# Attention with relative bias, then a sine-gated MLP: 64-row score pairs on a planned PSUM tile, and an output turned by DMA

## The chip, the cores and the metric

The kernel runs on one core of a Trainium2 chip. The metric is the device time of one execution in microseconds, as the median of several runs. Engines are named as in the profile: PE (TensorE, matmuls), PEld (its weight loads), DVE (VectorE), ACT (ScalarE), POOL (GpSimd), SP (SyncE, which only issues DMAs here).

## The reference

Eight batches of 576 tokens with eight heads of 64. Attention adds a bias that depends on the distance of two tokens alone; the heads side by side are the 512 features of 4,608 tokens, which pass through an MLP of width 2,048:

```python
scores = scale * np.matmul(q, k.transpose(0, 1, 3, 2)) + bias
attn = np.exp(scores - scores.max(-1)); attn = attn / (attn.sum(-1) + 1e-9)
x = np.matmul(attn, v)            # to (4608, 512)
h = x @ w_in
s = np.sin(alpha * h)
out = (h + s * s / (alpha + 1e-09)) @ w_out
```

The bias is constant from distance 128 on. The kernel multiplies the exponentials by exp(bias minus that constant) in a window near the diagonal alone, and leaves the maximum out, since the row sum divides it away.

## The kernel before

**Stages.** For each batch t there is an attention stage (ACT holds the table of the exponential) and an MLP stage (the table of the sine); `set_table` (L788) loads 1.28 us of table between them. MLP works on blocks b of 512 tokens, which don't line up with batches of 576; the last stage does blocks 7 and 8.

**Order.** Nothing is scheduled by hand in the code below `Plan` (L55). `plan_pair`, `plan_av`, `plan_moe_in` and `plan_mo` add tasks with the engines that can do them, an estimated duration, dependences, a priority, and the buffers they take or use. `Plan.run` (L94) is a list scheduler in model time: it picks the next task and emits its instructions at once. So its choices are fixed when the program is built; each engine then works through its own queue in that order and waits on semaphores. Tasks marked `fill` (the second MLP matmul) go where PE has room, up to a quota in the attention stage.

**Scores (`plan_pair`, L565).** Heads go in pairs p = 0..3; k and q of a pair stand in partitions 0 to 63 and 64 to 127. The matmuls use all 128 rows: `kzs` holds the pair's k twice, each time with the other head's half zeroed, so that a product with both heads' q gives one head's scores. Keys are cut into four chunks of 128 and a rest of 64 (for the rest, `kts` puts both heads into one 128-column operand). Queries are cut into windows w of 384 and 192 (`WIN`). A pair has seven units: four of 2 x 384 columns, one of 2 x 288 (the rest) and two of 4 x 192. A unit fills two PSUM banks (`new_sc(2)`); one ACT exponential (L606) takes it to `u` in SBUF. DVE multiplies the bias windows in (L618, L635).

**Output (`plan_av`, L646).** For each pair and window, per 128 queries 9 matmuls with `u` as weights and v as moving operand (65 columns per head, the 65th being ones, so that the row sum comes along; 130 for the rest keys). DVE divides (L677, L678) into `xn`, PE turns each 128x128 piece (L688), and DVE or ACT copies it to `xT` (L698), the MLP's operand: features in partitions, a ring of 1,536 tokens.

**MLP.** `plan_moe_in`: 16 times per block, 4 matmuls of 512 columns from `w_in` into a bank of `sc` (L720), sine on ACT (L727), its square on ACT or DVE (L734, L736), and the gate on DVE (L741) into `g`. `plan_mo`: 4 times 16 matmuls of `g` and `w_out` into `mo`, a copy to `outs`, and a store from SP (L782).

**PSUM.** Eight banks: four for `sc` (scores and h in turn), two `av` (output and its turn), two `mo`.

**Loads.** For t of 2 and more, POOL's queue copies k and q from fp32 to fp16 in DRAM (`stage_kq`, L332, two batches ahead), SP's queue loads them transposed (`load_kqT`, L339): k to `kraw`, from there with four more DMAs to `kzs` and `kts`, then q. v comes through POOL's queue (`load_v16`). These are emitted by `first` (L799) at the head of an attention stage, but SP and POOL run ahead as far as their waits let them. For batches 0 and 1, PE turns k and q (`plan_tr`, L498), and DVE or ACT copies them out (L494, L496), k in two halves.

All operations' helpers are at one line each: `full` (L408) issues nearly every matmul.

Of the kernel before, what the change touches and what calls it, by code (L numbers as in the profile page):

```python
# [33 lines left out]
LAT = {"PE": 0.2, "ACT": 0.18, "DVE": 0.18, "POOL": 0.2, "DMA": 0.0}  # L34
NBUF = {"sc": 4, "av": 2, "mo": 2, "u": 2, "g": 2, "s16": 3, "sq": 3, "outs": 5, "xn": 3}


class Task:
    def __init__(self, engs, emit, deps, pri, nb=0.0):
        self.engs, self.emit, self.deps, self.pri, self.nb = engs, emit, list(deps), pri, nb  # L40
        self.allocs = []
        self.s_only = self.fill = False
        self.end = self.eng = None


class Buf:
    def __init__(self, tag):
        self.tag, self.users = tag, []

# [5 lines left out]
class Plan:  # L55


    def __init__(self):
        self.tasks = []
        self.sin = self.in_qk = False  # L60
        self.used = self.share = 0
        self.warm = None
        self.rings = {k: [] for k in NBUF}

    def add(self, engs, emit, deps=(), pri=0, nb=0.0, new=(), use=(), after=()):
        t = Task(engs, emit, deps, pri, nb)
        t.after = list(after)
        t.allocs = list(new)
        for b in list(new) + list(use):
            b.users.append(t)  # L70
        self.tasks.append(t)
        return t

    def ready(self, t):
# [8 lines left out]
        taken = {}  # L83
        for b in t.allocs:
            ring, n = self.rings[b.tag], NBUF[b.tag]
            k = taken[b.tag] = taken.get(b.tag, -1) + 1
            if len(ring) + k >= n:
                for x in ring[k - n].users:
                    if x.end is None:
                        return None  # L90
                    r = max(r, x.end)
        return r

    def run(self, t0):  # L94
        free = {e: t0 for e in ("PE", "ACT", "DVE", "POOL")}
        todo = list(self.tasks)
        while todo:
# [3 lines left out]
            for t in todo:  # L101
# [6 lines left out]
                for e in t.engs:  # L108
# [3 lines left out]
                    if t.fill:  # L112
                        if self.in_qk and self.used >= OFFSET + QUOTA * self.share:
                            continue
                        cands[e].append((st + FILL_GAP, t))
                    else:
                        cands[e].append((st, t))
            for e, c in cands.items():
# [6 lines left out]
                if best is None or (st, fin) < best[:2]:  # L125
                    best = (st, fin, e, t)
            st, fin, e, t = best
            if e == "PE" and self.warm is not None and free[e] < WARM_END:
                ring = self.rings["mo"][-2:]
                b = Buf("mo")  # L130
                x = Task({}, None, [], 0)
                b.users.append(x)
                if st > free[e] + 0.5 and len(ring) == 2 and all(
                    y.end is not None and y.end <= free[e] for y in ring[0].users
                ):
                    self.warm()
                    free[e] += 0.43
                    x.end, x.eng = free[e], e
                    self.rings["mo"].append(b)
                    continue  # L140
            if t.fill:
                self.used += 1
                st -= FILL_GAP
                fin -= FILL_GAP
            for b in t.allocs:
                self.rings[b.tag].append(b)
            t.emit(e)
            t.end, t.eng = fin + LAT[e], e
            free[e] = fin
# [6 lines left out]
FILL_GAP = 0.0  # L156
QUOTA = 48
# [15 lines left out]
SLACK = {"PE": 0.02, "ACT": 0.02, "DVE": 0.02, "POOL": 0.02}  # L173
# [14 lines left out]
def kernel(  # L188
# [24 lines left out]
    XN = 1536  # L213
# [21 lines left out]
    kzs = [sgl.tile([128, NP, 2 * S], F16, name=f"kz{i}") for i in range(2)]  # L235
    kraw = sgl.tile([128, NP, S], F16, name="kraw")
# [52 lines left out]
    def new_u():  # L289
        return tp.tile([128, 9, S], F16, name="u", tag="u", bufs=NBUF["u"])  # L290
# [16 lines left out]
    banks = [0]  # L307
    halves = {}

    def new_sc(n):  # L310
        z = banks[0] // 2 % 2
        m, pool = halves.get(z, (0, None))
        if m != n:
            if pool is not None:
                pool.release()
            pool = tc.alloc_tile_pool(
                name=f"sc{banks[0]}", bufs=1, space=bass.MemoryType.PSUM,
                side="right" if z else "left", reuse_waits="tile",
            )
            halves[z] = (n, pool)  # L320
        banks[0] += n
        if n == 1:
            return pool.tile([128, 512], F32, name="sc", tag="sc", bufs=2)
        return pool.tile([128, 2, 512], F32, name="sc", tag="sc", bufs=1)

    def new_av():
        return ps.tile([128, 512], F32, name="av", tag="av", bufs=NBUF["av"])

    def new_mo():
        return ps.tile([128, 512], F32, name="mo", tag="mo", bufs=NBUF["mo"])  # L330
# [8 lines left out]
    def load_kqT(t):  # L339
        nc.sync.dma_start_transpose(out=kraw[:, :, :], in_=staged_k.ap()[t])  # L340
        kz = kzs[t % 2]
        nc.sync.dma_start(out=kz[0:64, :, 0:S], in_=kraw[0:64, :, :])
        nc.sync.dma_start(out=kz[64:128, :, S : 2 * S], in_=kraw[64:128, :, :])
        for z in range(2):
            r = slice(64 * z, 64 * z + 64)
            nc.sync.dma_start(out=kts[t % 2][r, :, r], in_=kraw[r, :, 512:S])
        nc.sync.dma_start_transpose(out=qTs[t % 2][:, :, :], in_=staged_q.ap()[t])
# [48 lines left out]
    def clear(eng, i):  # L396
        eng.memset(kzs[i][0:64, :, S : 2 * S], 0.0)
        eng.memset(kzs[i][64:128, :, 0:S], 0.0)
# [11 lines left out]
    def warm(n):  # L410
        x = new_mo()
        for _ in range(n):
            full(x, zz[:, 0:128], zz, True, True)
# [51 lines left out]
    eps_ = new_mo()  # L465
# [21 lines left out]
    plan.warm = lambda: warm(1)  # L487
# [10 lines left out]
    def plan_tr(t, p, kq, pri, nb, deps=()):  # L498
# [3 lines left out]
        def mm(e):  # L502
            c.v = new_mo().bitcast(F16)
# [15 lines left out]
        def cp(e):  # L519
            pin = c.v[:, 0:S].rearrange("d (i p) -> d p i", i=SI)  # L520

            def put(dst, r):
                copy_on(e, dst.rearrange("d (p i) -> d p i", i=SI)[r], pin[r])

            if kq == 1:
                put(qTs[t][:, p, :], slice(0, 128))
            else:
                put(kzs[t][:, p, 0:S], slice(0, 64))
                put(kzs[t][:, p, S : 2 * S], slice(64, 128))

        m = plan.add({"PE": 0.4 if t == 0 and p == 0 else 0.5}, mm, deps, pri, nb, new=[b])
        eng = {"DVE": 0.75, "ACT": 0.72} if kq else {"DVE": 1.6, "ACT": 1.55}
        if t == 0:
            eng = {"ACT": 0.72} if p == 0 and kq else {"DVE": eng["DVE"]}
# [4 lines left out]
        def tail(e):  # L539
            for z in range(2):  # L540
                r = slice(64 * z, 64 * z + 64)
                nc.vector.tensor_copy(  # L542
                    out=kts[t][r, p, r], in_=kzs[t][r, p, S * z + 512 : S * z + S]
# [4 lines left out]
    def plan_alpha():  # L548
        b, c = Buf("mo"), Cell()

        def mm(e):
            c.v = new_mo()
# [12 lines left out]
    def plan_pair(t, p, kqt, tails, first, gate, ub):  # L565

        u = Cell()
        done = {}
        units = [(0, c) for c in range(4)] + [(1, 0), (2, 0), (2, 2)]
        head = []  # L570
        for i, (kind, c) in enumerate(units):
            b, sc = [Buf("sc"), Buf("sc")], Cell()

            def qk(e, i=i, kind=kind, c=c, sc=sc):
                if i == 0:
                    if p == 0:
# [3 lines left out]
                plan.share = (len(units) * p + i + 1) / (NP * len(units))  # L580
                if p == NP - 1 and i == len(units) - 1:
                    plan.in_qk = False
                sc.v = new_sc(2)
                kz, qT = kzs[t % 2], qTs[t % 2]
                for z in range(2):
                    if kind == 1:
                        full(sc.v[:, z, 0:288], kts[t % 2][:, p, :],
                             qT[:, p, 288 * z : 288 * z + 288], True, True)
                        continue
                    for y in range(1 if kind == 0 else 2):  # L590
                        k0 = S * z + 128 * (c + y)
                        q0, n = WIN[0 if kind == 0 else 1]
                        full(sc.v[:, z, n * y : n * y + n], kz[:, p, k0 : k0 + 128],
                             qT[:, p, q0 : q0 + n], True, True)

            def ex(e, kind=kind, c=c, sc=sc):
                uz = u.v[:, 0:8, :].rearrange("p (z c) q -> p z c q", z=2)
                if kind == 0:
                    o, x = uz[:, :, c, 0:384], sc.v[:, :, 0:384]
                elif kind == 1:  # L600
                    o = u.v[:, 8, :].rearrange("p (b q) -> p b q", b=2)
                    x = sc.v[:, :, 0:288]
                else:
                    o = uz[:, :, c : c + 2, 384:576]
                    x = sc.v[:, :, 0:384].rearrange("p z (c q) -> p z c q", c=2)
                nc.scalar.activation(out=o, in_=x, func=AF.Exp, scale=0.125)  # L606

            base = PB + 100 * (16 * p + 2 * i)
            n = 576 if kind == 1 else 768
            m = plan.add({"PE": n / 2400.0 + 0.01}, qk, kqt + (tails if kind == 1 else []), base,  # L610
                         after=head, new=b + ([ub] if i == 0 else []))
            head = head or [m]
# [253 lines left out]
```

## Time and profile before

| what | us |
|---|---|
| median of three runs | 417.92 |
| the runs | 414.37, 417.92, 418.93 |
| span of the profiled execution | 410.3 |
| 32 outputs' turns on PE: 160 transposes, busy | 19.5 |
| xT copies on DVE (128x192 and 128x384), busy | 7.9 and 5.3 |
| xT copies on ACT (128x384 and 128x192), busy | 6.5 and 2.4 |
| products with the bias on DVE, L635 (192) and L618 (32), busy | 70.5 and 8.2 |
| score matmuls, busy: 384, 192 and 288 columns | 60.4, 31.4 and 13.0 |

The profiled execution has a span from its first to its last instruction; the time of a run has some us more around it. "Busy" of a group is the time in which at least one of its instructions ran, and matmuls overlap in their pipeline, so that a mean duration is longer than the distance between two of them. "Idle before" names what an engine waited for. A stage is the stretch between two table loads on ACT. A product L635 may cover both heads of a pair.

### The profile page before, as it was taken

The page shows a single profiled execution, that of the slowest core. Times are in us where ns is not written, and L with a number is a line of the kernel's source. Part 1 is how long each engine was busy: PE and PEld are TensorE (multiplying, and loading weights), DVE is VectorE, ACT ScalarE, POOL GpSimd, SP SyncE. Part 2 cuts the span into 40 slices and gives each one's busy share as a digit, 9 for nine tenths or more (in the row PEclk, how much of TensorE's full clock was granted, in tenths as well). Part 3 has the DMA queues.
Part 4 walks back from the last instruction along what each step waited for, and adds up shares of the span by engine and source line. Part 5 has one row for each costly group of instructions (what it writes and reads, how often), then busy time and mean ns, then how long its engine had stood idle before and what let it go on. Part 6 is the DMA issues. An engine that isn't in the chain of part 4 may idle for free.

```text
span 410.3 us, 8747 instructions
## 1 busy us (share of the span) xinstructions
PE 395.4 (96%) x3519; PEld 227.5 (55%) x3519; DVE 289.7 (71%) x683; ACT 337.3 (82%) x502; POOL 85.6 (21%) x98
## 2 busy tenths in 40 slices
PE   4897999999999999999999999999999999999996
PEld 1474446754576447744665467645764477444442
DVE  5895996749666976688576956696768766799200
ACT  2877988879988998889888998799979988899311
POOL 7863952044000900071004400120000000000000
PEclk9999999999999999999999999999999999999999
DMA  9899999949900995099906990293000000000111
GB/s 170 189 206 219 205 162 158 216 89 164 185 28 29 155 182 94 27 135 165 131 28 104 161 142 27 69 169 79 27 28 27 26 27 27 28 1 0 53 77 77
DMA packets 135145, 41.90 MB, mean 102 GB/s; under 512 B 121209, under 2 KB 129489, under 8 KB 135105
## 3 DMA queue, kind: packets, MB, share of 16 engines
q0 software_dynamic: 89872, 19.04, 54.5%
q1 hardware_dynamic: 45008, 22.26, 24.2%
q8 instruction: 27, 0.44, 0.4%
q14 instruction: 14, 0.11, 0.1%
q10 hardware_dynamic: 224, 0.05, 0.1%
HBM read 37.76 MB, written 16.52 MB: 132 GB/s over the span
## 4 chain that ended last, share of the span: by engine, by line
PE 88%; DVE 8%; DMA 1%; ACT 1%; issue 1%; ACTq 0%; DVEq 0%
PE sc L408 44%; PE mo L408 30%; PE av L408 11%; PE av L688 2%; DVE kz L496 2%; DVE g L741 2%; DMA phi_sb<-phi_const 1%; DVE u L635 1%; DVE xn L678 1%; DVE qT L496 1%; ACT u L606 1%; DVE kt L542 1%; DVE sq L736 0%; PE mo L507 0%; PE mo L513 0%
## 5 line engine op out<-in xcount | busy, mean ns | idle before, releaser
L606 ACT ACTIVATE u<-sc 128x768 f16<-128x768 f32 (+1 forms) x224 | 165.9, 788 | 28.6 <-PE sc L408 23.5
L408 PE MATMUL mo<-w_out,g 128*128 128x512 f16 x576 | 156.5, 379 | 0.0
L408 PE MATMUL sc<-xT,w_in 128*128 128x512 f16 x576 | 131.2, 379 | 0.5 <-DVE g L741 0.5
L741 DVE SCALAR_TENSOR_TENSOR g<-sq,inv_a,sc 128x512 f16<-128x512 f16 x144 | 104.7, 747 | 7.8 <-ACT sq L734 4.9
L727 ACT ACTIVATE s<-sc,alphaT 128x512 f16<-128x512 f32 x144 | 92.4, 677 | 8.4 <-PE sc L408 7.3
L408 PE MATMUL sc<-qT,kz 128*128 128x192 f16 (+1 forms) x512 | 89.5, 288 | 2.0 <-ACT qT L494 0.7
L408 PEld LDWEIGHTS <-w_in 128*128 128x128 f16 x576 | 55.3, 98 | 64.7 <-issue 0.8
L635 DVE TENSOR_TENSOR u<-u,m2r 128x512 f16<-128x512 f16 (+1 forms) x192 | 70.5, 388 | 17.4 <-ACT u L606 14.9
L408 PEld LDWEIGHTS <-g 128*128 128x128 f16 x576 | 55.8, 98 | 45.2
L408 PEld LDWEIGHTS <-u 128*128 128x128 f16 x1440 | 55.2, 97 | 10.6 <-ACT u L606 2.5
L352 POOL DMA_DIRECT2D v<-in_v_dram x24 | 22.2, 1064 | 163.7 <-PE av L408 163.7
L408 PE MATMUL av<-v,u 128*128 128x65 f16 x1280 | 54.9, 193 | 0.5 <-DVE u L635 0.5
L408 PEld LDWEIGHTS <-kz 128*128 128x128 f16 x512 | 42.6, 98 | 22.0 <-issue 4.4
L734 ACT ACTIVATE sq<-s 128x512 f16<-128x512 f16 x79 | 49.4, 629 | 2.3
L677 DVE RECIPROCAL rd<-av 128x6 f32<-128x6 f32 x64 | 12.0, 188 | 38.1 <-PE av L408 38.1
L408 PE MATMUL av<-vh,u 128*128 128x130 f16 x160 | 35.2, 220 | 0.1
L678 DVE TENSOR_TENSOR xn<-av,rd 128x384 f16<-128x384 f32 x64 | 31.4, 491 | 2.2
L736 DVE TENSOR_TENSOR sq<-s 128x512 f16<-128x512 f16 x65 | 27.3, 421 | 2.9 <-ACT s L727 2.5
L496 DVE COPY outs<-mo 128x512 f32<-128x512 f32 x27 | 18.6, 690 | 10.9 <-PE mo L408 10.7
L688 PEld LDWEIGHTS <-xn 128*128 128x128 f16 x160 | 13.6, 98 | 18.0 <-DVE xn L678 6.4
L494 ACT ACTIVATE outs<-mo 128x512 f32<-128x512 f32 x9 | 5.4, 597 | 20.7 <-PE mo L408 20.7
L688 PE MATMUL av<-id_sb,xn 128*128 128x128 f16 x160 | 19.5, 220 | 2.9 <-DVE xn L678 2.8
(68 smaller groups left out, 185.6 us busy)
## 6 DMA issues: line engine op xcount, KB each, us to landing
out_dram<-outs SPq DMA_DIRECT2D x36, 256.0 KB, 2.0
staged_k<-in_k_dram POOLq DMA_DIRECT2D x6, 576.0 KB, 11.2
staged_q<-in_q_dram POOLq DMA_DIRECT2D x6, 576.0 KB, 17.5
kz<-kraw SPq DMA_DIRECT2D x12, 288.0 KB, 7.0
v<-in_v_dram POOLq DMA_DIRECT2D x24, 128.0 KB, 6.0
w_in<-in_moe_w_in_dram POOLq DMA_DIRECT2D x4, 512.0 KB, 8.5
w_out<-in_moe_w_out_dram POOLq DMA_DIRECT2D x4, 512.0 KB, 10.8
w_out<-in_v_dram SPq DMA_DIRECT2D x4, 256.0 KB, 9.1
```

The lines of the kernel that those rows point to most:

```text
L352: nc.gpsimd.dma_start(out=vs[t % 2][:, c, :, 0:D], in_=vp[128 * c : 128 * c + 128],)
L408: nc.tensor.matmul(out=out, lhsT=lhsT, rhs=rhs, start=start, stop=stop)
L496: k_of(e).tensor_copy(out=o, in_=i)
L606: nc.scalar.activation(out=o, in_=x, func=AF.Exp, scale=0.125)
L635: nc.vector.tensor_tensor(out=io, in0=io, in1=m2[:, 2 * p : 2 * p + 2, x0 : x0 + hi - lo], op=ALU.mult,)
L677: nc.vector.reciprocal(out=r, in_=a[:, :, :, D])
L678: nc.vector.tensor_tensor(out=xn.v[:, 0:nq].rearrange("p c (z d) -> p c z d", z=2), in0=a[:, :, :, 0:D], in1=r.unsqueeze(3).to_broadcast([ ...
L688: nc.tensor.transpose(out=tr.v[:, qc - q0 : qc - q0 + 128], in_=xn.v[:, i], identity=id_sb)
L727: nc.scalar.activation(out=s16.v, in_=h.v, func=AF.Sin, scale=alphaT[:, f : f + 1])
L734: nc.scalar.activation(out=sq.v, in_=s16.v, func=AF.Square)
L736: k_of(e).tensor_tensor(out=sq.v, in0=s16.v, in1=s16.v, op=ALU.mult)
L741: nc.vector.scalar_tensor_tensor(out=gcell[b].v[:, f, :], in0=sq.v, scalar=inv_a[:, f : f + 1], in1=h.v, op0=ALU.mult, op1=ALU.add,)
```

## The change

- **Scores.** `kzs` and `kraw` go; `kTs` holds k once. A score matmul takes 64 rows: head 0's in partitions 0 to 63 and head 1's in 64 to 127, into two banks, one after the other in the queue. The first window of scores is 512 queries wide, the second 64. Units: A (one chunk, 2 x 512 columns), C (the rest keys, as before at full height), and B (the last 64 queries of two pairs, all chunks: 16 matmuls of 64 columns). Per group g of two pairs: eight A, two C, one B.
- **Runs.** The score matmuls of up to three units become one PE task (`plan_att`). In batch 0 each unit is a run of its own.
- **PSUM.** One tile of eight banks, `pb`, whose banks the plan gives out: pairs (0,1), (2,3), (4,5) to score units, single banks 0 to 5 to h and to turns on PE, 6 and 7 to both `av` and `mo`.
- **Turn by DMA.** From batch 1 on, pairs 0 to 2 are turned by SP's DMA transposes from `xn` straight to `xT`: one for a first window, two for a second. Batch 0 and pair 3 stay on PE. `xn` has 6 buffers instead of 3. `xT`'s ring is 1,728 tokens; the first MLP matmul of a block that wraps is issued in two pieces.
- **Loads.** k and q are loaded by two DMA transposes with no copies between; the rest keys go to `kts` by two POOL copies (`load_kt`). v, k, q of t+1 and the staging of t+2 are emitted with the table load that ends attention t.
- Model durations of some tasks are other ones.

```diff
-LAT = {"PE": 0.2, "ACT": 0.18, "DVE": 0.18, "POOL": 0.2, "DMA": 0.0}
-NBUF = {"sc": 4, "av": 2, "mo": 2, "u": 2, "g": 2, "s16": 3, "sq": 3, "outs": 5, "xn": 3}
+LAT = {"PE": 0.2, "ACT": 0.18, "DVE": 0.18, "POOL": 0.2, "SP": 2.4}
+NBUF = {"u": 2, "g": 2, "s16": 3, "sq": 3, "outs": 5, "xn": 6}
+PAIRS = ((0, 1), (2, 3), (4, 5))
+BANKS = {"h": (0, 1, 2, 3, 4, 5), "av": (6, 7), "mo": (7, 6)}
...
-    XN = 1536
+    XN = 3 * S
...
-        nc.sync.dma_start_transpose(out=kraw[:, :, :], in_=staged_k.ap()[t])
-        kz = kzs[t % 2]
-        nc.sync.dma_start(out=kz[0:64, :, 0:S], in_=kraw[0:64, :, :])
-        nc.sync.dma_start(out=kz[64:128, :, S : 2 * S], in_=kraw[64:128, :, :])
+        nc.sync.dma_start_transpose(out=kTs[t % 2][:, :, :], in_=staged_k.ap()[t])
+        nc.sync.dma_start_transpose(out=qTs[t % 2][:, :, :], in_=staged_q.ap()[t])
+
+    def load_kt(t):
         for z in range(2):
             r = slice(64 * z, 64 * z + 64)
-            nc.sync.dma_start(out=kts[t % 2][r, :, r], in_=kraw[r, :, 512:S])
-        nc.sync.dma_start_transpose(out=qTs[t % 2][:, :, :], in_=staged_q.ap()[t])
+            nc.gpsimd.tensor_copy(out=kts[t % 2][r, :, r], in_=kTs[t % 2][r, :, 512:S])
...
-                put(kzs[t][:, p, 0:S], slice(0, 64))
-                put(kzs[t][:, p, S : 2 * S], slice(64, 128))
+            dst = (kTs, qTs)[kq][t][:, p, :]
+            copy_on(e, dst.rearrange("d (p i) -> d p i", i=SI), pin)
...
+            for x0, pp, cc, qs in todo:
+                for z in range(2):
+                    r = slice(64 * z, 64 * z + 64)
+                    full(sc.v[:, z, x0 : x0 + qs.stop - qs.start],
+                         kT[r, pp, 128 * cc : 128 * cc + 128], qT[r, pp, qs], True, True)
...
+        runs = ([(a, "A", 0), (a, "A", 1), (a, "A", 2)], [(a, "C", 0)],
+                [(a, "A", 3), (b, "A", 0), (b, "A", 1)], [(b, "C", 0)],
+                [(b, "A", 2), (b, "A", 3), (b, "B", 0)])
+        if t == 0:
+            runs = [[x] for r in runs for x in r]
...
+        if t > 0 and p < NP - 1:
+
+            def turn(e):
+                for i, r0, m in ((0, 0, 384),) if w == 0 else ((0, 0, 128), (1, 64, 64)):
+                    k = -(-m // 128)
+                    nc.sync.dma_start_transpose(
+                        out=xT[:, p, x0 + 128 * i : x0 + 128 * i + m].rearrange(
+                            "d (c q) -> d c q", c=k),
+                        in_=xn.v[r0:128, i : i + k, :].rearrange("p c d -> p (c d)"),
+                    )
+
+            return [plan.add({"SP": 0.3 + 0.3 * w}, turn, [x], base, use=[xb])]
...
-            if 1 <= t < T - 1:
-                load_v16(t + 1)
-                load_kqT(t + 1)
-            if t + 2 < T:
-                stage_kq(t + 2)
+            if t == 0:
+                stage_kq(2)
...
+        def swap(e, t=t):
+            set_table(SIN_SET)
+            if 1 <= t < T - 1:
+                load_v16(t + 1)
+                load_kqT(t + 1)
+                if t + 2 < T:
+                    stage_kq(t + 2)
+                load_kt(t + 1)
```

## The prediction

> **What bounds the kernel now.** I read the page's busy shares and its chain of waits first, then the table of stages (cut at the activation table loads, which mark where the exponentials end and the sines begin), then the chain in order of time, the groups by shape, and the transfers.
>
> ```profile
> span 410.3 us, 8747 instructions
> PE 395.4 (96%) x3519; PEld 227.5 (55%) x3519; DVE 289.7 (71%) x683; ACT 337.3 (82%) x502; POOL 85.6 (21%) x98
> ...
> PE 88%; DVE 8%; DMA 1%; ACT 1%; issue 1%; ACTq 0%; DVEq 0%
> ```
>
> TensorE is busy 96% of the span and carries 88% of the chain that ended last. ScalarE at 82% is the next one.
>
> ```profile
> 0.00:36.65 36.65, 28.51 (x350) 17.29 (x350) 28.13 (x77) 24.33 (x36) 24.84 (x41) 1.00 1.00 190
> 36.65:58.64 21.99, 20.16 (x187) 9.69 (x185) 18.30 (x38) 19.82 (x34) 15.07 (x19) 1.00 1.55 200
> ...
> 174.22:192.22 18.00, 18.00 (x104) 8.65 (x102) 15.58 (x29) 16.54 (x27) 9.24 (x8) 1.00 1.49 147
> 192.22:217.99 25.77, 25.77 (x301) 17.39 (x299) 16.83 (x48) 22.55 (x31) 0.00 (x0) 1.00 0.64 80
> ...
> 349.43:410.30 60.87, 57.21 (x284) 26.16 (x281) 30.70 (x54) 35.72 (x58) 0.00 (x0) 1.00 0.10 40
> ```
>
> Columns: stretch, its length, then busy time of PE, weight loads, DVE, ACT and POOL, then the granted clock (1.00 everywhere). In steady state one batch is an MLP stage of 18.00 us and an attention stage of 25.77, 43.77 together; PE has no gap in either. ACT works 16.54 + 22.55 = 39.09 us of it. So time goes only where PE work goes, until ACT takes over.
>
> ```profile
> 178.77 5.18 PE sc L408 x24
> ...
> 197.43 0.92 PE av L408 x27
> 198.34 0.66 PE sc L408 x6
> ```
>
> These pieces of the chain give what a matmul really costs in a stream (the mean durations overlap). 24 of 512 columns take 5.18 us: 0.216 each. Six score matmuls (two of 384 columns, four of 192: 1,536) take 0.66 us: 0.43 ns a column. An attention-output run of 24 x 65 + 3 x 130 columns takes 0.92, or 0.034 a matmul.
>
> **PE: scores.** Per batch now 32 matmuls of 384 columns, 32 of 192 and 8 of 288: 20,736 columns x 0.43 ns = 8.9 us. After: 16 pairs of 512, 16 pairs of 64 and the 8 of 288. If the two matmuls of a pair run at once, 8,192 + 1,024 + 2,304 = 11,520 columns = 5.0 us. Saved: 3.9 us a batch. If they run one after the other, the columns are 20,736 again and nothing is saved. No row here shows two matmuls at once: the trace's rows, all at full height, speak for serial. I take the overlap, because a pair's matmuls use different partition halves and different banks, and keep the serial case as a rival. [...]
>
> The 64-column matmuls are short: at 0.034 each 16 pairs cost 0.54 us instead of the 0.44 that 1,024 columns give, or 1.09 if weights have to be loaded one after the other. I add 0.25.
>
> **PE: change of tile height.** In the built order of a batch after the first there are 6 stretches of 64-row matmuls between full-height ones, and 10 in batch 0: 52 stretches, 104 changes. The trace has none. Bounds: nothing, or as much as a start from scratch, where the weight load at 196.43 is followed by its matmul at 196.72, 0.29 us. A mean 512-column matmul lasts 0.379 against its pitch of 0.216, so 0.163 is filling and draining, most of which a stream hides. I take 0.1 a change, nearer to that; 1.2 us a batch. [...]
>
> **PE: turning the output.** Three of four head pairs, from batch 1 on, lose 5 PE transposes of 128 columns each: 15 x 128 x 0.43 ns = 0.8 us a batch. Sum on PE: -3.9 + 0.25 + 1.2 - 0.8 = -3.3, so 43.8 becomes 40.5. Beside it, xT's ring of 1,728 tokens makes MLP blocks 3 and 6 wrap, with 64 more matmuls each; from 0.216 for 512 columns and 0.034 for 65 (0.41 ns a column) a matmul has 0.0075 of its own: 128 x 0.0075 = 1.0 us in all.
>
> **ACT, the next limit.**
>
> ```profile
> L606 ACT ACTIVATE u<-sc 128x768 f16<-128x768 f32 x192 | 148.6, 811 | 28.6 <-PE sc L408 23.5 <-ACT u L606 2.3
> L606 ACT ACTIVATE u<-sc 128x576 f16<-128x576 f32 x32 | 20.8, 651 | 0.0
> ...
> 193.51 4.55 ACT L606 ACTIVATE u<-sc 128x768 f16<-128x768 f32 x6
> ```
>
> Six exponentials in 4.55 us are 0.758 each. The two shapes differ by 160 ns for 192 columns, 0.833 ns a column, so 0.64 is columns and 0.118 is the price of an instruction. 24 of 768 become 18 of 1,024, the same columns: 6 x 0.118 = 0.7 saved. ACT's xT copies (6.5 + 2.4 us in the trace, 1.1 a batch) lose three quarters: 0.8. ACT falls from 39.1 to 37.6 us, against a PE of 40.5. Before, ACT stood idle 4.7 us a batch; now only 2.9 would be left. If all the 4.7 are needed (table loads at the turn of the stages, the first scores), the period is 42.3. Also the scores now come three units at a time in six banks, and the attention outputs share two banks with the MLP output instead of having two each, so PE can meet a held bank. I put 0.5 between: **41.0 us**, 2.8 less. DVE loses six products and its share of xT copies from 32.4 us; it is not late next.
>
> **Ends of the program.** Batch 0: 4 pairs of k copies of 1.54 us (two halves) become single ones of 0.76 as for q; 3.1 us on DVE in a chain that also waits for the bias window and for v. I take 2 (0 to 4). First MLP stage: four such copies for batch 1, shared by DVE and ACT: 1.5 of 21.99 (0 to 3). Clearing of the padded k goes from POOL (4.0 us) and DVE (2.0); both wait for DMAs there, nothing counted.
>
> **Transfers.**
>
> ```profile
> kraw<-staged_k SPq DMA_TRANSPOSE x6, 7.6
> qT<-staged_q SPq DMA_TRANSPOSE x6, 11.3
> ```
>
> SP now issues 9 transposes of xn a batch, between the stores and the loads of k and q. Each of the largest (128x384) moves a sixth of a 576x512 one. Landing: below 7.6 us if size counts; a 256 KB store lands in 2.0, so 2 to 7.6, and I take 3. The built order of PE puts between the output of pair 2 (first window) and the first MLP matmul: a score run (0.85), 16 MLP-output matmuls (3.5), 27 + 36 output ones (2.1) and three turns (0.2), 6.6 us, less some 1.2 for division and its waits: **5.4 us** of cover. 3 is hidden. The second windows aren't needed by their own batch's MLP from batch 2 on. In batch 1 they are, and stand behind the k and q transposes on SP, whose issue took 4.15 and 6.33 us there: 10.5 less the cover of 5.4 and some MLP-output matmuls. I add 3 us once (0 to 6). Stores and POOL's v loads queued behind have no reader within a stage; k's small copies move from SP (some 2 us a batch) to POOL, where only the next batch's loads wait. Loading k and q a batch later leaves them the 18 us of one MLP stage; today's chain from 220.51 to the landing of q (231.66 + 8.54 and its tail) is 20, of which 4 go with the kz copies. Hidden with little left.
>
> **Sum.** Batch 0 -2, first MLP -1.5, batch 1 -2.8 + 3, five periods -14, last attention stage (25.77 of 43.77) -1.6, last stage 0 (it is MLP work alone), wrapped blocks +1.0: -17.9. Span 392.4. Outside of the span lie 417.92 - 410.3 = 7.6 us, as before: **400 us**, 4.3% less.
>
> **Rivals.**
> - *PE's gain is eaten (pairs serial, or a change near 0.29):* serial, the 3.9 come back in each of some 6.5 periods: 25 us, span 417.4, 425 us. With 0.29, 104 x 0.19 = 20 us more: 412.4, 420 us. For it: the trace knows only full-height rows. Against: nothing is shared within a pair, and 0.29 is a start after a wait. 420 to 425, 10%.
> - *ACT or banks become the limit:* period 42.3: 1.3 x 6.5 = 8.5 more, 409 us. For it: ACT at 93% of 40.5. Against: 64 MLP-output matmuls a batch fill PE's waits, and all stand in the attention stage. 20%.
> - *The turn lands late (slower):* xn's transposes land like q's, 11.3 us, beside the staging of k and q, cut into rows of 64 elements. Place: the first matmul of each MLP stage, with PE's whole queue behind it and ACT's sines behind that. 11.3 - 5.4 = 5.9, x 7 = 41: span 433, 441 us. It is slower from a landing of 8.0 us on (5.4 plus 17.9 / 7). For it: both large transposes landed at 7.6 or above. Against: a sixth of the size, in a stage that moves 80 GB/s. 8%.
> - *Better than said:* a change of height costs nothing and there is no new wait: period 39.3, 1.7 x 6.5 = 11 less, and batch 1's 3 us hidden: 386 us. 12%.
>
> My forecast has 50%. Below 1%, about 4 us, a measurement of this kernel can't tell from no change. Faster by more than that: forecast 0.50, better 0.12, ACT's case 0.19 of 0.20: 0.81; within it: 0.01 of ACT's and half of the eaten case, 0.06; slower: the late turn and the other half, 0.13. The range, 385 to 415, goes from the better case to ACT's case with the ends' bounds (409, and part of the 3.5 us at the start and 3 in batch 1); it leaves out the eaten case and the late turn, 0.18.
>
> **What would show it.** Right: score groups of 128x512 whose pairs start together and a stretch of six that lasts about 0.65 us plus two changes; 144 exponentials of 1,024 near 0.97; periods between table loads of 41.0; no wait of PE for xT but in batch 1. Wrong: a wait of the first MLP matmuls for a DMA of xT, pairs 0.43 apart, or PE gaps of more than 1 us an attention stage before ACT or a bank.

## The result, and the profile after

| | before | after |
|---|---|---|
| median of four runs on one chip, us | 418.43 (414.37 to 419.08) | 393.48 (392.17 to 395.04) |
| span of the profiled execution | 410.3 | 391.9 |
| its time | not recorded | 393.65 |
| period of a batch (MLP and attention stage), mean of five | 43.80 | 40.82 |

The ratio is 0.945, 95% interval 0.939 to 0.952. The page of the changed kernel: its span, busy times, chain by engine, and the granted clock in 40 slices.

```profile
span 391.9 us, 8874 instructions
...
PE 373.4 (95%) x3542; PEld 203.3 (52%) x3542; DVE 269.2 (69%) x602; ACT 317.1 (81%) x431; POOL 87.2 (22%) x108
...
PEclk8579989989999999999999999999999999999999
...
PE 82%; DVE 7%; DMA 5%; ACT 3%; issue 1%; POOL 1%; SPq 1%; ACTq 0%; DVEq 0%
```

TensorE is still the bound, with 22 us less busy time. Of the chain, 5% is DMA now, which was 1%. The stages, cut at the table loads as before (length, busy PE, weight loads, DVE, ACT, POOL, then clock, DMA share and GB/s):

```profile
0.00:30.19 30.19, 25.40 (x294) 13.97 (x294) 21.29 (x57) 22.68 (x28) 19.90 (x37) 0.72 1.03 197
30.19:50.92 20.73, 17.97 (x163) 9.49 (x162) 17.21 (x37) 17.23 (x29) 13.73 (x17) 1.00 1.23 211
50.92:74.65 23.73, 22.75 (x301) 12.83 (x301) 18.15 (x48) 21.68 (x26) 7.01 (x6) 0.93 2.18 152
74.65:103.47 28.82, 24.04 (x163) 11.69 (x161) 15.61 (x31) 16.95 (x29) 9.96 (x10) 0.94 1.30 127
103.47:125.19 21.72, 21.72 (x247) 11.73 (x246) 14.37 (x36) 20.59 (x23) 0.00 (x0) 1.00 0.17 51
185.41:206.99 21.58, 21.26 (x244) 11.50 (x243) 14.23 (x36) 20.58 (x23) 0.00 (x0) 1.00 0.80 92
206.99:226.15 19.16, 19.16 (x148) 9.89 (x146) 16.30 (x33) 15.98 (x26) 10.06 (x10) 1.00 1.25 138
...
329.29:391.90 62.61, 58.81 (x330) 27.67 (x327) 30.69 (x58) 34.48 (x57) 0.00 (x0) 1.00 0.12 41
```

A steady attention stage went from 25.77 to 21.6 us, a steady MLP stage from 18.0 to 19.2: some of PE's work slid past the last exponential, and only their sum counts. One row stands out: the MLP stage of batch 1 takes 28.82 us, 4.8 of them without PE work. Before it took 18.96:

```profile
85.60:104.56 18.96, 18.21 (x104) 8.69 (x102) 15.08 (x28) 16.73 (x28) 9.22 (x8) 1.00 1.83 142
```

The stage ahead of it, the attention stage of batch 1 (50.92 to 74.65), has a clock of 0.93: PE ran at half clock from 55.4 to 58.9 us, behind waits for the copies of batch 1's k (the longest 1.26 us). In the kernel before, the clock reads 1.00 there.

The groups by shape show the new score work (busy, mean ns, idle before):

```profile
L609 ACT ACTIVATE u<-pb 128x1024 f16<-128x1024 f32 x144 | 137.4, 1027 | 10.2 <-PE pb L425 9.5
L425 PE MATMUL pb<-qT,kT 64*128 64x512 f16 x256 | 41.0, 411 | 0.7 <-ACT u L609 0.6
L425 PE MATMUL pb<-qT,kT 64*128 64x64 f16 x256 | 6.6, 193 | 0.0
```

256 matmuls of 512 columns are busy for 41.0 us, 0.160 each, where a full-height one has a pitch of 0.216: they overlap. The 144 exponentials of 1,024 columns are busy for 137.4 us, 0.954 each (0.97 forecast). PE waits 0.6 us in the whole run for ACT to free a score bank. The timeline of PE in a steady stage (start, length, engine, line, operation, count):

```profile
184.78 1.24 PE L425 MATMUL pb<-w_out,g 128*128 128x512 f16 x5
185.96 0.82 PE L425 MATMUL pb<-qT,kT 64*128 64x512 f16 x6
186.71 1.25 PE L425 MATMUL pb<-w_out,g 128*128 128x512 f16 x5
...
193.48 0.84 PE L425 MATMUL pb<-qT,kT 64*128 64x512 f16 x20
194.25 1.04 PE L425 MATMUL pb<-w_out,g 128*128 128x512 f16 x4
```

Starts are read here, not lengths: matmuls overlap, and the five from 184.78 on show a length of 1.24 us at a pitch of 0.216. Five full-height matmuls at 0.216 from 184.78 end their turn at 185.86; the scores start at 185.96: 0.10 us for the change of height. Three pairs, 0.65 us at 0.216 a pair, would give way at 186.61; the next matmul starts at 186.71: 0.10 again. The last row pair is a run whose third unit is the 64-column one (20 matmuls): 0.77 us, hardly more than the 0.75 of three ordinary units. What the MLP of batch 1 waits for is seen on SP, which issued its DMAs in this order, and on PE:

```profile
77.03 2.93 SPq L360 DMA_TRANSPOSE kT<-staged_k  x1
80.06 2.62 SPq L361 DMA_TRANSPOSE qT<-staged_q  x1
82.77 0.53 SPq L851 DMA_DIRECT2D out_dram<-outs  x1
83.40 2.39 SPq L745 DMA_TRANSPOSE xT<-xn  x2
```

```profile
86.73 14.93 PE L425 MATMUL pb<-xT,w_in 128*128 128x512 f16 x62 [4.48 <-DMA xT<-xn]
```

The turn of pair 2's second window is issued behind the k and q transposes for batch 2, and PE waits 4.48 us for it. After the gap 62 matmuls take 14.93 us, where 62 x 0.216 is 13.4: PE ran at half speed at first (the granted clock from 87.0 to 89.5 is 0.50). ACT stood idle for 6.89 us before the first sine.

### The profile page after: what moved, and what is told of

Same layout as the page of the kernel before. It is cut to its first block, busy times and chain, and to the rows that moved or that the text cites. A ratio compares the mean times of both kernels' runs of the same rounds, so it can differ in the third digit from the quotient of the medians.

```text
span 391.9 us, 8874 instructions
## 1 busy us (share of the span) xinstructions
PE 373.4 (95%) x3542; PEld 203.3 (52%) x3542; DVE 269.2 (69%) x602; ACT 317.1 (81%) x431; POOL 87.2 (22%) x108
## 4 chain that ended last, share of the span: by engine, by line
PE 82%; DVE 7%; DMA 5%; ACT 3%; issue 1%; POOL 1%; SPq 1%; ACTq 0%; DVEq 0%
PE pb L425 81%; DMA m2r<-e_dram 2%; DVE u L628 2%; DVE xn L733 2%; DVE g L810 1%; DMA e_dram<-e_sb 1%; ACT u L609 1%; DMA phi_sb<-phi_const 1%; DMA xT<-xn 1%; ACT s L796 1%; PE pb L757 1%; DVE sq L805 1%; DVE qT L512 1%; SPq L361 0%; DVE rd L732 0%
## 5 line engine op out<-in xcount | busy, mean ns | idle before, releaser
L609 ACT ACTIVATE u<-pb 128x1024 f16<-128x1024 f32 (+1 forms) x176 | 154.6, 962 | 10.3 <-PE pb L425 9.5
L425 PE MATMUL pb<-w_out,g 128*128 128x512 f16 x576 | 139.3, 381 | 0.0
L425 PE MATMUL pb<-xT,w_in 128*128 128x512 f16 (+4 forms) x704 | 128.3, 343 | 4.5 <-DMA xT<-xn 4.5
L796 ACT ACTIVATE s<-pb,alphaT 128x512 f16<-128x512 f32 x144 | 93.3, 680 | 21.3 <-PE pb L425 20.3
L810 DVE SCALAR_TENSOR_TENSOR g<-sq,inv_a,pb 128x512 f16<-128x512 f16 x144 | 100.6, 742 | 4.8 <-ACT sq L803 3.2
L425 PE MATMUL pb<-v,u 128*128 128x65 f16 x1280 | 55.8, 195 | 0.0
L425 PE MATMUL pb<-qT,kT 64*128 64x64 f16 (+1 forms) x512 | 45.1, 302 | 0.7 <-ACT u L609 0.6
L425 PE MATMUL pb<-vh,u 128*128 128x130 f16 x160 | 35.5, 222 | 2.3 <-DVE xn L733 1.8
L733 DVE TENSOR_TENSOR xn<-pb,rd 128x384 f16<-128x384 f32 (+1 forms) x64 | 31.4, 491 | 2.2
L425 PEld LDWEIGHTS <-kT 64*128 64x128 f16 x512 | 16.9, 96 | 21.6 <-issue 13.8
L858 ACT ACT_TABLE_LOAD x15 | 19.2, 1283 | 0.3
```

Source lines behind the costliest of these rows:

```text
L425: nc.tensor.matmul(out=out, lhsT=lhsT, rhs=rhs, start=start, stop=stop)
L733: nc.vector.tensor_tensor(out=xn.v[:, 0:nq].rearrange("p c (z d) -> p c z d", z=2), in0=x[:, :, :, 0:D], in1=r.unsqueeze(3).to_broadcast([ ...
L796: nc.scalar.activation(out=s16.v, in_=h.v, func=AF.Sin, scale=alphaT[:, f : f + 1])
L810: nc.vector.scalar_tensor_tensor(out=gcell[b].v[:, f, :], in0=sq.v, scalar=inv_a[:, f : f + 1], in1=h.v, op0=ALU.mult, op1=ALU.add,)
L858: nc.scalar.preload_act_table_set(name)
```

## The experiments

Each was run beside the kernel before on the same chip; medians before were 415.25 (first four experiments), 415.39 (next four) and 414.67 (last two). So medians of different groups are compared by their ratios.

**1. Do the pairs overlap, and what does a change of height cost?** Two kernels with the same order of instructions. The first puts both matmuls of a pair into the same 64 partitions:

```diff
-                    r = slice(64 * z, 64 * z + 64)
+                    r = slice(0, 64)
```

> Both matmuls of a score pair read partitions 0 to 63, so that they can't run at once (the second head's scores are taken from the first head's operands). Same order, same number of changes of height. Theory A (pairs overlap, and that is where the time came from): 144 units get 0.216 us longer, 31 us on PE, of which the seven full batches show about 27: near 420 us, periods near 44.5. Theory B (PE was not what the change relieved, or pairs didn't overlap): 394 us.

The second uses all 128 rows, so that there is neither overlap nor change of height (`slice(0, 128)` in the same place).

> The score matmuls of A and B units read all 128 partitions (each score is then the sum over both heads), so PE never changes its tile height; pairs run one after the other as in e1. Theory A (a change of height costs 0.1 us, 0.2 a stretch, and PE is the limit): 104 changes, about 10 us less than e1, near 410 us. Theory B (a change costs nothing that shows): the same as e1. Theory C (0.29 a change): 30 us less than e1.

With 64 rows one after the other: 424.36 us, ratio 1.022 (1.014 to 1.031), period 44.56. With 128 rows: 411.35 us, ratio 0.992 (0.987 to 0.996), period 43.31. PE in a steady stage, 64 rows first, then 128:

```profile
203.91 1.47 PE L425 MATMUL pb<-qT,kT 64*128 64x512 f16 x6
205.31 1.25 PE L425 MATMUL pb<-w_out,g 128*128 128x512 f16 x5
```

```profile
192.62 1.03 PE L425 MATMUL pb<-w_out,g 128*128 128x512 f16 x4
193.49 1.46 PE L425 MATMUL pb<-qT,kT 128*128 128x512 f16 x6
194.78 1.24 PE L425 MATMUL pb<-w_out,g 128*128 128x512 f16 x5
```

At full height the six hold PE from 193.49 to 194.78, 1.29 us, which is 6 x 0.216, with no step on either side (192.62 + 4 x 0.216 = 193.48). At 64 rows the same six take 1.40: 0.10 for the way back. By whole periods: the overlap is worth 44.56 - 40.82 = 3.74 us a batch, and 12 changes of height cost 44.56 - 43.31 = 1.25, 0.104 each. The medians lie 13.0 us apart, more than seven periods give; some 6 of these arose in the first stage (37.30 against 31.33 us), where the profile with 64 rows had a slow PE for longer (see the last section). So the period is the clean measure, not the total. The three prices add up: 3.74 - 1.25 and 0.74 for the turn (next experiment) are 3.23 us a batch, of 2.98 measured; the rest of the change thus costs about 0.25. In each steady attention stage PE waits some 0.3 us for an output bank that a division has yet to read (1.8 us in the whole run):

```profile
202.71 0.22 PE L425 MATMUL pb<-vh,u 128*128 128x130 f16 x1 [0.32 <-DVE xn L733]
```

**2. The turn by DMA.** All turns on PE (`if False:` in place of the condition), and turns by DMA from batch 2 on:

```diff
-        if t > 0 and p < NP - 1:
+        if t > 1 and p < NP - 1:
```

> All turns of the attention output stay on PE, with copies by DVE and ACT; no DMA transposes of xn. Theory A (the DMA turn saves 0.8 us a batch on PE and loses about 6 in batch 1, where its second window stands behind the loads of k and q): both cancel, 391 to 396 us, and no gap of PE ahead of the first MLP matmul of batch 1. Theory B (the DMA turn is a clear gain of the change): 399 us or more.

> Turns by DMA from batch 2 on only; batch 1 is turned on PE. Theory A (the wait of 4.5 us in batch 1's MLP, and the half clock after it, come from the DMA turn): 5 to 6 us less than the changed kernel, near 388. Theory B (batch 1 is late for another reason, such as loads that land late): 393 to 395, with a gap in the same place.

All on PE: 391.28 us, ratio 0.944 (0.938 to 0.949); period 41.56, which is 0.74 more, and no wait for xT in batch 1. From batch 2 on: 388.22, ratio 0.936 (0.930 to 0.942), period 40.91, no such wait. So the turn by DMA gains 0.74 us in each later batch, some 4.4 in six, and batch 1 alone loses as much again: the change as it is would be no slower without it (ratios 0.944 and 0.945).

**3. Is it the place in SP's queue?** Same turns, same order on PE; only loads move. In one kernel the loads for batch 2 are emitted with the first sine of block 1, that is behind batch 1's turns (edit below); in the other the loads of every batch go to the head of the attention stage, where they were before the change.

```diff
             def sn(e, f=f, h=h, s16=s16):
+                if b == 1 and f == 0:
+                    load_next(1)
...
-            if 1 <= t < T - 1:
-                load_v16(t + 1)
...
-                load_kt(t + 1)
+            if t != 1:
+                load_next(t)
```

> Turns as in the changed kernel; only the loads for batch 2 (k, q, v, staging of batch 3) are emitted with the first sine of batch 1's MLP, so that on SP they stand behind the turns of batch 1's second window and not ahead. PE's order stays the same. Theory A (place on SP's queue): the wait of 4.5 us and the half clock after it go, 5 to 6 us less than the changed kernel, near 388, as in e4. Theory B (a DMA turn at that moment is slow by itself, or batch 2's loads then come late): 393 or more.

> The loads of batch t+1 and the staging of t+2 are emitted at the head of attention t, as before the change. Theory A (moving them to the MLP stage matters, because on SP the turns of a batch would stand behind them and they would land beside the staging): later turns, a few us more, 395 to 400. Theory B (SP and POOL run ahead of the emission anyway, and batch 1's second window is then no longer behind a load): same or up to 6 us less, 388 to 394.

Behind the turns: **386.98 us**, ratio 0.932 (0.929 to 0.935), the best of all kernels here. Its windows (columns as above) and SP's order:

```profile
75.49:98.28 22.79, 22.49 (x163) 11.41 (x161) 15.59 (x31) 16.96 (x28) 9.49 (x10) 1.00 0.87 112
98.28:120.00 21.72, 21.72 (x247) 11.73 (x246) 14.36 (x36) 20.59 (x23) 0.48 (x1) 1.00 0.97 102
```

```profile
80.19 2.38 SPq L745 DMA_TRANSPOSE xT<-xn  x2
82.68 2.83 SPq L360 DMA_TRANSPOSE kT<-staged_k  x1
85.60 3.09 SPq L361 DMA_TRANSPOSE qT<-staged_q  x1
```

The MLP stage of batch 1 falls from 28.82 to 22.79 us, PE's idle time in it from 4.8 to 0.3, and the period stays 40.82. At the head: 397.88, ratio 0.957 (0.952 to 0.961), and in its trace the q transpose blocks SP for longer still, ahead of all of batch 1's turns:

```profile
63.60 8.52 SPq L361 DMA_TRANSPOSE qT<-staged_q  x1
72.23 1.21 SPq L745 DMA_TRANSPOSE xT<-xn  x1
```

Its PE first waits 3.33 us for a division that itself waits for a buffer of xn, which the late turns hold, and then 5.63 us for xT; the stage takes 35.1 us, 10.2 of them at half clock. Its period is 40.82 too. Both show that the stall is a matter of SP's order in batch 1 alone.

**4. Runs of three units.** Every unit a run of its own in all batches (`if t == 0:` becomes `if True:`, with the priorities that batch 0 uses).

> Every score unit is a run of its own in all batches, as in batch 0, instead of up to three to a run. Theory A (each stretch of 64-row matmuls costs 0.2 us to enter and leave): up to 12 more stretches a batch in seven batches, less those that stand together, so up to 17 us more, 400 to 410. Theory B (runs of three matter little, or shorter runs feed ACT better and win that back): 390 to 396.

407.34 us, ratio 0.982 (0.978 to 0.986). In the whole run there are 103 stretches of 64-row matmuls instead of 52; its span is 404.0, 12.1 us more than that of the changed kernel, or 0.119 for each of 102 more changes. By the ratios (0.982 and 0.945) it is 15.2 us, or 0.149. Both are upper bounds on a change, since the order of the work differs too. Its period, 41.23, hides this: 203 instead of 134 MLP-output matmuls were left for the last stage, which takes 77.4 us. That is 1.7 to 2.2 us a batch over seven batches, of the 3.74 - 1.25 = 2.5 that the pairs net: without the grouping some 70 to 90% of it would go.

**5. The first stage.** It became 6.5 us shorter (36.65 to 30.19), where the prediction said 2. First idea: more buffers for the exponentials' output, tried in the kernel before (`"u": 4, "outs": 4`).

> The kernel before, with room for four pairs of u (the changed kernel holds four: two buffers of two pairs) instead of two; outs has four buffers instead of five to make room. Theory A (batch 0 ended its exponentials 6.5 us earlier because they needn't wait for the output of the pair two before, which waits for v and the bias windows): first table load to the sine 3 to 5 us earlier, 411 to 415 where before is at 415 to 418. Theory B (batch 0's gain is the single copy of k and fewer exponentials): same as before.

416.55 us, ratio 1.002 (0.999 to 1.004): no gain. (Its first stage is 38.53 us, but with PE at half clock for another 3.4 us, from 20.5 to 23.9, so the ratio is the measure.) Second idea: the copies of k. In the changed kernel k of batches 0 and 1 is again copied in halves, beside the changed kernel as it is:

```diff
-            copy_on(e, dst.rearrange("d (p i) -> d p i", i=SI), pin)
+            for r in ((slice(0, 64), slice(64, 128)) if kq == 0 else (slice(0, 128),)):
+                copy_on(e, dst.rearrange("d (p i) -> d p i", i=SI)[r], pin[r])
...
-        eng = {"DVE": 0.75, "ACT": 0.6}
+        eng = {"DVE": 0.75, "ACT": 0.6} if kq else {"DVE": 1.6, "ACT": 1.55}
...
```

> The changed kernel with one thing put back: for batches 0 and 1 a pair's k is copied out of PSUM in two copies of 64 partitions, as before, with the old model durations (1.6 and 1.55 us). The result is the same; the built order of the first two stages changes a little. The question is why the first stage (to the first load of the sine's table) became 6.5 us shorter (36.65 to 30.19), where the prediction said 2. Theory A, DVE: before, the chain of waits of the first stage ran along DVE's copies of k and q from 12.4 to 19.3 us, and only then came the products with the bias; 4 copies of 0.75 us less are 3 us less there. Put back, the first stage takes 33 to 35 us, and the kernel 2.5 to 5 us more than the changed one beside it (up to 1.5 of it in the first MLP stage). Theory B, the copies stand beside other work (the chain of the changed kernel's first stage waits for the bias window's DMA until 21.65 us): the first stage stays at 30 to 31.3 us and the kernel within 1 us of the changed one.

> The changed kernel as it is, on the same chip and in the same rounds as the run with two copies, for the comparison: 391 to 395 us, first stage 30 to 31.3, MLP stage of batch 1 28 to 29 us. If its first stage differs from 30.19 by more than 1 us, stages of single profiles can't be compared that closely.

396.32 us (396.05 to 396.64) against 393.75 (391.35 to 395.85): 2.6 us, or 1.7 by the spans of the two profiles (394.0 and 392.3). By the medians the cost lies just within theory A's bounds, by the spans below them, and it isn't in its place: the first stage took 28.70 us with two copies and 30.92 without. So the length of the first stage isn't a measure of the copies. In the profile with two copies PE had its full speed from about 14 us on, in the two of the changed kernel from 24.7 and 25.2 (an output's nine matmuls take 0.30 us at full speed, 0.54 before: 0.033 and 0.060 each). The cost appears later: the MLP stage of batch 0 takes 21.88 instead of 20.52 us and the attention stage of batch 1 26.78 instead of 23.83. There PE waits for copies of batch 1's q, up to 1.90 us at a time, and runs at half clock for 10.2 us (51.7 to 61.9) where the changed kernel does for 3.4 (55.9 to 59.4). Another 6.8 us at half clock can cost 3.4 us (half of it, an estimate from the clock), more than the whole difference, and the earlier full speed in the first stage works the other way. So the price of the copies by themselves is open. Nor does it end with the same work done. The counts of MLP-output matmuls and the outputs of batch 0 show this; here the MLP stage of batch 1, before and after:

```profile
L408 PE MATMUL mo<-w_out,g 128*128 128x512 f16 x15 | 4.2, 379 | 0.0
```

```profile
L425 PE MATMUL pb<-w_out,g 128*128 128x512 f16 x31 | 7.6, 379 | 0.0
```

By the start of that stage the kernel before had done 58 MLP-output matmuls, the changed one 40: 18 x 0.216 = 3.9 us of PE work come later, 16 of them in this stage. And at the first table load the kernel before had divided seven of batch 0's eight outputs, the changed one four. Only where as much work is done can times be compared: at the end of batch 1's MLP stage (73 and 71 matmuls).

## Why the prediction was right, and where its terms were off

Predicted 400 us with 385 to 415; measured 393.48. The likeliest case came true: PE stayed the limit, the pairs overlap, a change of height costs about 0.1 us, and ACT, banks and the steady batches' turns hold nothing up for long.

| term of the sum | predicted | measured | from |
|---|---|---|---|
| to the end of batch 1's MLP stage, without a stall (-2 - 1.5 - 2.8) | -6.3 | -7.1 | 104.56 before, 103.47 - 6.0 after |
| stall in batch 1 | +3 (0 to 6) | +6.0 | its stage: 28.82 - 22.79 in the kernel without the stall |
| five periods | -14 | -14.9 | 5 x (43.80 - 40.82) |
| last attention stage and last stage | -1.6 and 0 | -4.2 and +1.7 | 25.89 to 21.72 (batch 2's stage, as the five periods run from its end), 60.87 to 62.61 |
| two blocks that wrap | +1.0 | 0.3, within the periods | stages of 19.29 and 19.28 against 19.12 and 19.16 |
| span | 392.4 | 391.9 | |
| outside of the span | 7.6 | 1.75 | 393.65 - 391.9 |

The stall took 3.0 us more than forecast, the other terms together 3.5 less; that the span fits to 0.5 us is partly luck.

- **Pairs overlap.** Right, and shown: 3.9 us a batch forecast, from an overlap that no row of before shows and that the author assumed; 3.74 by the run with the pairs in series. The rival of 425 us is close to what that run gave (424.36, beside a kernel before of 415.25).
- **Change of height.** 0.1 us forecast, a choice between bounds of 0 and 0.29 and not worked out, so the close fit is in part luck; 0.10 on either side in the trace, 0.104 by the periods, at most 0.119 to 0.149 by the run with single units. The runs put it below the 0.163 us by which the mean duration of a 512-column matmul (0.379) exceeds its pitch (0.216).
- **64-column pairs.** Mis-sized: 0.25 us a batch forecast, about nothing measured (0.77 us for a run with them, 0.75 without). Less one change and two pairs of 512, eight 64-column pairs took 0.24 us, 0.030 a pair: no wait for weights shows.
- **Turn on PE.** 0.8 us a batch forecast, 0.74 by the run with all turns on PE. A transpose from `xn` landed after 2.6 us in the median (2.2 to 8.8), where 3 was assumed, and no stage but batch 1's waited for one.
- **ACT and banks.** Period forecast 41.0, of which 0.5 for new waits; 40.82, with 0.3 a batch for the output banks. PE waited 0.6 us for ACT's scores in the run, so the case of 409 us did not arise. One reason given against it was read wrongly: the MLP-output matmuls don't all stand in the attention stage (51 did before, and 15 in the MLP stage; after, 51 and 16).
- **Batch 1's second windows.** The mechanism was right (behind k and q on SP) and shown by moving the loads either way; the size was 6.0 instead of 3. (Between the ends of the two profiles' stages lie only 5.2 us, because the kernel without the stall came to that stage 0.84 us later.) Missing were the half-speed matmuls after the gap (14.93 - 13.4 = 1.5 us). The wait itself, 4.48, came from terms that were off in both directions: k and q held SP for 2.93 and 2.62 us, not 4.15 and 6.33, and the cover was not 5.4 us. Pair 2's last division ended at 78.51; without the wait PE would have gone on at 82.25, 3.7 us later; but the turn was issued at 83.40 and let PE go on at 86.73. That the wait is near the forecast of 3 is in part luck.
- **k copies.** 3.5 us forecast for both batches, 1.7 to 2.6 measured, with the half clock in it that the forecast didn't have. Yet the first two batches gained 7.1 instead of 6.3: about 1 to 2 us came from elsewhere. What shortened the first stage to 30 us beyond work put off isn't settled; the moment at which PE reached full speed differs from profile to profile and blurs it.
- **Outside of the span.** The largest miss of the number, 5.8 us: 417.92 was the median of three runs, 410.3 the span of another execution, and their difference isn't time outside a span. In each later profile the time exceeds the span by 1.75 to 2.6 us (416.46 and 414.7 for a kernel before with more buffers), in the runs of the kernel before by 1.7 to 1.9. The profiled execution of before was thus some 6 us faster than the median, within the spread that the kernel has (410.7 to 419). With 1.8 in place of 7.6 the same sum gives 394.2.

## What to carry to other kernels

Where two products of 64 rows can stand in different halves of the array, pair them, and group the pairs so that a stretch is long against 0.2 us for both its changes of height: six matmuls here save 0.65 us for 0.2. When a step moves from a compute engine to a DMA queue, list what is issued ahead of it in the one batch that differs from the steady ones: a transpose of a whole batch held its queue for 2 to 8.5 us here, and putting those of one batch behind the small ones added about a quarter to the gain (ratios 0.932 and 0.945). A span is compared with a span; a stage is compared only where the same work has been done by its end.

## What the runs showed of the hardware

In the first stage PE ran at about half its later speed where the granted clock reads 1.00. In the kernel with 64 rows in series, that stage has

```profile
27.10 2.74 PE L425 MATMUL pb<-qT,kT 64*128 64x512 f16 x6
```

that is 0.44 us a matmul against 0.23 in the same kernel at 203.91, and the clock from 27 to 30 us reads 1.00. That 1.00 is no measurement: the trace's record of the clock begins at 33.15 us in this kernel, with full speed (an output's nine matmuls take 0.54 us at 23.56 and 0.31 at 33.25), and a window ahead of the first record reads 1.00. In the kernel before the record begins at 13.96 us, so the 1.00 that the prediction reads there for the first stage is wrong up to that time (384 columns have a pitch of 0.31 us from 12.73 on, 0.165 in the steady stages). In the changed kernel's own profile it begins at 4.24, and the stretch from 7.65 to 24.7 us is on record with 0.50. Ahead of the first record the pitch of equal matmuls is the only witness. Full speed came to stay in the first stage at 13.96 us in the profile of before, at 24.7 in that of after, and at 33.15 in the kernel in series. Stretches at half clock on record lasted 3.41 us twice in the profile of after (from 55.44 and 86.16) and 17.07, five times that, from 7.65; with two copies of k they lasted 6.8 (from 7.3) and 10.2 (from 51.7), two and three times that. In the kernel in series PE was busy without a gap from 9 us on, and slow for 24 us more. About the end of the wait of 4.48 us (86.73) the clock was at half for 3.41 us, from 86.16 to 89.57. What decides the moment at the start was not found.

Two DVE copies of 64x64 from SBUF to SBUF took 0.37 us together in most places of the changed kernel's profile, and 2.46 in one:

```profile
13.69 2.46 DVE L552 COPY kt<-kT 64x64 f16<-64x64 f16 x2
```

In both profiles of the changed kernel the long ones (2.46 and 2.40) ended where POOL began to issue its next DMA (16.15 and 16.12; 17.29 and 17.27), after POOL's casts; in the kernel with the loads behind the turns, too (1.96 long; 17.23 and 17.21). Whether the two engines hold each other up was not tried.
